# Windowed attention and two mixture layers on one core: gating products pinned in VectorE's queue, two a step, then four

## The chip, the core and the metric

The kernel runs on one core of a Trainium2 chip. The core has five engines with a queue of their own each: TensorE (PE in the rows; PEld is its weight load), VectorE (DVE), ScalarE (ACT), GpSimd (POOL) and SyncE (SP), which here issues nearly all DMA transfers. An engine takes its queue in order. The metric is device microseconds from start to end, the median of several runs.

## The reference

Three stages follow each other on 2304 tokens (4 sequences of 576) of 512 values:

```python
# 1. attention, 8 heads of 64: row i sees columns i-63 .. i
scores = where((rel >= 0) & (rel < 64), q @ k.T / 8, -1e9)
x = softmax(scores) @ v                      # tokens x 512
# 2. phase one: 512 -> 2048 -> 512
h = x @ w_in
g = where(h >= 1, h, where(h <= -1, 0, (h + 1)**2 / 4))
x = g @ w_out
# 3. phase two: 8 experts, each 512 -> 1024 -> 512, one for a token
logits = x @ w_gate                          # tokens x 8
e = argmax(logits); p = softmax(logits)[e]
out = p * (maximum(x @ w1[e], 0) @ w2[e])
```

## The kernel before

**Precision.** Matrices are split into a high and a low part, `hi` and `lo`; a product is three passes (hi hi, hi lo, lo hi), so that each operand needs a conversion on ScalarE and a subtraction on VectorE or GpSimd.

**Phase one.** Tokens lie in seven blocks of 256 or 384. A step is one of 16 slices of 128 hidden values for one block: `layer1` (L435), 12 products at L440 into the PSUM tile `h`, of which there are two; `act_g` (L447), a chain of six passes by turns on ScalarE and VectorE: L449 (ScalarE), L450 (VectorE), L451 (ScalarE), L452 (VectorE, the last that reads `h`), L455 (ScalarE, `ghi`), L456 (VectorE, `glo`); and, two steps later, `layer2` (L471), nine products at L475. The code walks over steps in the loop at L990. A step has two slots, `run_slot` at L1002 and L1021, into which other work is put: attention of later blocks, and what follows.

**Phase two.** All tokens are first sent through one expert, the one chosen most often among the first 128 tokens (`choose`, L607: its number `pi` goes to SyncE, which then loads that expert's weights as `er`; L642 converts them on ScalarE, L643 subtracts on GpSimd). Six blocks of 384 tokens take eight steps each: `layer1`, then `act_relu` (L461) with L464 on ScalarE and L465 on VectorE, then `layer2`, and `evac2` (L653), which scales with the gate's weight `GW` on ScalarE (L657) and writes to the output. `prep` (L901) fetches each block's input transposed (`tt`), joins its halves in `xj` and splits it (L910 on ScalarE, L911 on GpSimd). Tokens that belong to another expert are gathered after `route` and `pick` (L660, L724), put through their own expert (weights `wl`, again L642 and L643; first product L784), and scattered over the output.

**The gating products.** Logits are made on VectorE, one product of 128 tokens with one column of `w_gate` at a time: 18 tiles x 8 experts = 144 calls of `gate_logit` (L565), each a multiply with a running sum (`junk`) and a read of the accumulator (`Lg`); the trace has both under L569. The first call of a tile loads its rows, `xg`, of which two buffers exist. `gate_until(s, n)` (L928) puts the next n products into slot s; behind a tile group's last product follow `gate_finish` (L589), behind the first tile's also `choose`, and behind the last tile's `route` and `pick`. Slots from the start of phase one's last block get three products at first (RATE0), then two (RATE1, and RATE2 in phase two); a step has two slots, so four a step.

**What sets the order.** The code's order is not the queues' order. A scheduler reorders each engine's instructions when the program is built, by its own estimate of when inputs are there. A product needs only its rows and `w_gate`, so it can move up to where those are thought to have landed: in the queue before, products fill gaps between the passes of the activation chains of earlier steps as well.

Of the kernel before, what the change touches and what calls it, by code (L numbers as in the profile page):

```python
# [30 lines left out]
FAR = 32768.0  # L31
MAXT = NTILE + E - 1
RATE0 = 3
RATE1 = 2
RATE2 = 2
LA = 0
SPN = 8
# [73 lines left out]
def kernel(  # L111
# [14 lines left out]
    nc = tc.nc  # L126
# [423 lines left out]
    def load_rows(t, tag):  # L550
        r = Z["p2"].tile([P, DM], F32, tag=tag, name=tag, bufs=2)
        nc.sync.dma_start(r, x2s[t * P:t * P + P])
        return r
# [11 lines left out]
    def gate_logit(t, e):  # L565
        if e == 0:
            xg[t] = load_rows(t, "xg")
        junk = Z["p2"].tile([P, DM], BF16, tag="junk", name="junk")
        nc.vector.tensor_tensor_reduce(  # L569
            out=junk, in0=xg[t], in1=Z["wgb"][:, e], scale=1.0, scalar=0.0,  # L570
            op0=ALU.mult, op1=ALU.add, accum_out=Z["L"][:, t, e:e + 1],
        )

    def first_max(src, dst, n):

# [301 lines left out]
    def at(s, fn, *a):  # L877
        slots.setdefault(s, []).append((fn, a))
# [39 lines left out]
    sl = base + 2 * seg0[NB - 1]  # L918
# [9 lines left out]
    def gate_until(s, n):  # L928

        for t, e in gq[:n]:  # L930
            at(s, gate_logit, t, e)
            if e == E - 1:
                if t == 0:
                    at(s, gate_finish, 0, 1)
                    at(s, do_choose)
                elif t % TB == TB - 1:
                    a0 = max(1, t - TB + 1)
                    at(s, gate_finish, a0, t + 1 - a0)
                if t == NTILE - 1:
                    at(s, route)  # L940
                    at(s + 1, do_pick)
        del gq[:n]

    e0 = base + 2 * S2
    for s in range(sl + 1, e0):
        gate_until(s, RATE0 if s < sl + 5 else RATE1)
    for s in range(e0, e0 + 2 * KF2 * (NB2 - 1)):
        gate_until(s, RATE2)
    assert not gq
# [81 lines left out]
    with tc.For_i(1, n_left, 1):  # L1031
        nc.vector.tensor_scalar(out=Z["pos"], in0=Z["pos"], scalar1=-float(P), scalar2=None, op0=ALU.add)
        nc.vector.tensor_scalar(out=Z["j"], in0=Z["j"], scalar1=1.0, scalar2=None, op0=ALU.add)
        ev, idx, s, xl = pick()
# [65 lines left out]
```

## Time and profile before

| | us |
|---|---|
| median of three runs (772.76, 773.0, 776.55) | 773.0 |
| the profiled execution | 774.57 |
| its span, first to last instruction | 772.8 |
| TensorE busy | 727.8 (94%) |
| VectorE busy | 519.5 (67%) |
| ScalarE busy | 417.3 (54%) |
| GpSimd busy | 207.3 (27%) |
| gating products on VectorE, 144 | 113.9 |

TensorE is busy for most of the span, so time is lost or won where it stands still or runs at its lower clock. The shares are means over stages: the last block of phase one lies at about 465 to 541 us, phase two from there to about 760. "Idle before" in a row is the time that an engine stood before the instructions of a group, and behind the arrow stands what ended that wait.

### The profile page before, as it was taken

The page shows a single profiled execution, that of the slowest core. Times are in us where ns is not written, and L with a number is a line of the kernel's source. Part 1 is how long each engine was busy: PE and PEld are TensorE (multiplying, and loading weights), DVE is VectorE, ACT ScalarE, POOL GpSimd, SP SyncE. Part 2 cuts the span into 40 slices and gives each one's busy share as a digit, 9 for nine tenths or more (in the row PEclk, how much of TensorE's full clock was granted, in tenths as well). Part 3 has the DMA queues.
Part 4 walks back from the last instruction along what each step waited for, and adds up shares of the span by engine and source line. Part 5 has one row for each costly group of instructions (what it writes and reads, how often), then busy time and mean ns, then how long its engine had stood idle before and what let it go on. Part 6 is the DMA issues. An engine that isn't in the chain of part 4 may idle for free. (4 is left out here: it accounts for less than half of the span.)

```text
span 772.8 us, 12584 instructions
## 1 busy us (share of the span) xinstructions
PE 727.8 (94%) x4507; PEld 635.4 (82%) x4507; DVE 519.5 (67%) x1163; ACT 417.3 (54%) x1031; POOL 207.3 (27%) x164
## 2 busy tenths in 40 slices
PE   6698999999999999999999999979999999899996
PEld 3587878888888899888988898768988988799885
DVE  5887988548777668865797398999979854111110
ACT  4777766576656767575677444555533335441212
POOL 2466643204421024300320001561220116520000
PEclk7599999999999999999999999999999999999999
DMA  8446830143432324532343314432353134510101
GB/s 322 158 144 211 281 117 27 56 143 102 146 108 91 117 62 121 152 90 76 82 157 83 149 28 136 145 115 55 127 86 99 33 99 121 155 35 14 42 1 52
DMA packets 66691, 83.78 MB, mean 108 GB/s; under 512 B 35671, under 2 KB 41559, under 8 KB 66498
## 3 DMA queue, kind: packets, MB, share of 16 engines
q1 hardware_dynamic: 66466, 82.52, 34.6%
q8 instruction: 36, 0.59, 0.3%
q0 software_dynamic: 160, 0.43, 0.2%
q14 instruction: 29, 0.24, 0.1%
HBM read 60.74 MB, written 14.42 MB: 97 GB/s over the span
## 5 line engine op out<-in xcount | busy, mean ns | idle before, releaser
L440 PE MATMUL h<-xT,wi 128*128 128x384 f32 (+1 forms) x1344 | 233.5, 322 | 15.8 <-DVE a L452 12.8
L440 PEld LDWEIGHTS h<-xT,wi 128*128 128x128 f32 x1344 | 211.4, 193 | 30.3 <-DVE a L452 21.3
L475 PE MATMUL acc<-wo,ghi 128*128 128x512 f32 x576 | 155.7, 398 | 0.3 <-ACT ghi L455 0.2
L475 PEld LDWEIGHTS acc<-wo,ghi 128*128 128x128 f32 x576 | 104.3, 190 | 16.7 <-ACT ghi L455 1.0
L569 DVE CUSTOM_DVE_ANT_0 junk<-xg,wgb 128x512 bf16<-128x512 f32 x144 | 113.9, 791 | 2.4 <-DMA xg<-x2s 0.6
L440 PE MATMUL h<-xT,we 128*128 128x384 f32 x576 | 110.9, 337 | 3.2 <-DVE glo L465 3.2
L440 PEld LDWEIGHTS h<-xT,we 128*128 128x128 f32 x576 | 102.0, 188 | 9.0 <-DVE glo L465 4.7
L465 DVE SCALAR_TENSOR_TENSOR glo<-h,ghi 128x384 fp32r<-128x384 f32 x48 | 26.6, 554 | 93.2 <-ACT ghi L464 93.2
L475 PE MATMUL acc<-wo,glo 128*128 128x512 f32 x288 | 85.9, 395 | 0.6 <-DVE glo L456 0.5
L475 PE MATMUL acc<-we,ghi 128*128 128x512 f32 x288 | 79.3, 395 | 2.3 <-ACT ghi L464 2.2
L451 ACT ACTIVATE a<-a 128x384 f32<-128x384 f32 (+1 forms) x112 | 53.0, 474 | 50.6 <-DVE a L450 50.3
L456 DVE TENSOR_TENSOR glo<-a,ghi 128x384 fp32r<-128x384 f32 (+1 forms) x106 | 64.8, 612 | 21.4 <-ACT ghi L455 20.6
L455 ACT ACTIVATE ghi<-a 128x384 fp32r<-128x384 f32 (+1 forms) x112 | 53.0, 475 | 42.9 <-DVE a L452 42.0
L449 ACT ACTIVATE a<-h,half 128x384 f32<-128x384 f32 (+1 forms) x112 | 58.8, 525 | 30.5 <-PE h L440 29.1
L452 DVE TENSOR_TENSOR a<-h,a 128x384 f32<-128x384 f32 (+1 forms) x112 | 55.5, 497 | 26.1 <-ACT a L451 25.1
L450 DVE TENSOR_SCALAR a<-a 128x384 f32<-128x384 f32 (+1 forms) x112 | 48.9, 437 | 26.3 <-ACT a L449 26.1
L475 PEld LDWEIGHTS acc<-wo,glo 128*128 128x128 f32 x288 | 53.2, 188 | 13.5 <-DVE glo L456 1.9
L464 ACT ACTIVATE ghi<-h 128x384 fp32r<-128x384 f32 x48 | 23.1, 484 | 75.6 <-PE h L440 63.1
L475 PEld LDWEIGHTS acc<-we,ghi 128*128 128x128 f32 x288 | 52.8, 188 | 10.9 <-ACT ghi L464 2.4
L264 POOL TENSOR_TENSOR qs<-qk,qs 64x512 fp32r<-64x512 f32 x16 | 21.8, 1364 | 132.7 <-ACT qs L257 99.7
L911 POOL TENSOR_TENSOR xT<-xj,xT 128x256 fp32r<-128x256 f32 x36 | 30.5, 855 | 86.8 <-ACT xT L910 86.8
L643 POOL TENSOR_TENSOR we<-er,we 128x512 fp32r<-128x512 f32 x16 | 24.1, 1515 | 95.3 <-ACT we L642 95.3
(170 smaller groups left out, 979.8 us busy)
## 6 DMA issues: line engine op xcount, KB each, us to landing
qk<-in_qk_dram SPq DMA_DIRECT2D x21, 640.0 KB, 3.9
vt<-in_vv_dram SPq DMA_DIRECT2D x32, 256.0 KB, 2.8
er<-in_w_dram SPq DMA_DIRECT2D x32, 256.0 KB, 2.9
wraw<-in_wi_dram SPq DMA_DIRECT2D x14, 512.0 KB, 4.5
wraw<-in_wo_dram SPq DMA_DIRECT2D x14, 512.0 KB, 6.0
xg<-x2s SPq DMA_DIRECT2D x18, 256.0 KB, 2.7
out_dram<-y SPq DMA_DIRECT2D x18, 256.0 KB, 2.3
qk<-in_qq_dram SPq DMA_DIRECT2D x11, 320.0 KB, 3.2
```

The lines of the kernel that those rows point to most:

```text
L440: nc.tensor.matmul(h[:, :n], w[:, wa, k * P:k * P + P], x[:, xa, k, :n], start=(i == 0), stop=(i == 3 * KD - 1),)
L449: nc.scalar.activation(a[:, :n], h[:, :n], ACTF.Relu, scale=0.5, bias=half[:, 0:1])
L450: nc.vector.tensor_scalar(out=a[:, :n], in0=a[:, :n], scalar1=1.0, scalar2=None, op0=ALU.min)
L451: nc.scalar.activation(a[:, :n], a[:, :n], ACTF.Square)
L452: nc.vector.tensor_tensor(out=a[:, :n], in0=h[:, :n], in1=a[:, :n], op=ALU.max)
L455: nc.scalar.activation(hi[:, :n], a[:, :n], ACTF.Copy)
L456: (nc.gpsimd if pool else nc.vector).tensor_tensor(out=lo[:, :n], in0=a[:, :n], in1=hi[:, :n].bitcast(F32), op=ALU.subtract)
L465: nc.vector.scalar_tensor_tensor(out=lo[:, :n], in0=h[:, :n], scalar=0.0, in1=hi[:, :n].bitcast(F32), op0=ALU.max, op1=ALU.subtract,)
L475: nc.tensor.matmul(a, ga[:, t * P:t * P + P], w[:, wa], start=(first and j == 0), stop=(last and j == 2),)
L569: nc.vector.tensor_tensor_reduce(out=junk, in0=xg[t], in1=Z["wgb"][:, e], scale=1.0, scalar=0.0, op0=ALU.mult, op1=ALU.add, accum_out=Z["L ...
L643: nc.gpsimd.tensor_tensor(out=w[:, 1], in0=raw, in1=w[:, 0].bitcast(F32), op=ALU.subtract)
L911: (nc.vector if 2 * t + i in PL_V else nc.gpsimd).tensor_tensor(out=lo, in0=r, in1=hi.bitcast(F32), op=ALU.subtract)
```

## The change

Three edits. RATE1 falls from 2 to 1, so a step of phase one's last block gets two products instead of four; the slots that get three are one fewer (nine products instead of twelve). RATE2 stays at 2, four a step in phase two. And each product is pinned: `keep_in_program_order` gives it an edge of order, without a wait, to the instruction that the code issued last on VectorE. It can't move up past that one any more, but instructions that the code issues later may still move ahead of it.

```diff
-RATE1 = 2
+RATE1 = 1
 RATE2 = 2
@@ gate_logit
-        nc.vector.tensor_tensor_reduce(
+
+        tc.keep_in_program_order(nc.vector.tensor_tensor_reduce(
             out=junk, in0=xg[t], in1=Z["wgb"][:, e], scale=1.0, scalar=0.0,
             op0=ALU.mult, op1=ALU.add, accum_out=Z["L"][:, t, e:e + 1],
-        )
+        ))
...
     for s in range(sl + 1, e0):
-        gate_until(s, RATE0 if s < sl + 5 else RATE1)
+        gate_until(s, RATE0 if s < sl + 4 else RATE1)
     for s in range(e0, e0 + 2 * KF2 * (NB2 - 1)):
         gate_until(s, RATE2)
```

Behind the added empty line, line numbers of the kernel after are one higher from L569 on. No instruction of the five engines is added or removed by it but those that wait.

In VectorE's queue, before, one step in the middle of phase one's last block reads as follows. Each product is two rows, `junk,Lg` and `Lg`; L450, L452 and L456 are the step's activation chain.

```order
L450 TENSOR_SCALAR a<-a 128x384
L569 ISA junk,Lg<-xg,wgb 128x512
L569 ISA Lg 128x1
L452 TENSOR_TENSOR a<-h,a 128x384
L569 ISA junk,Lg<-xg,wgb 128x512
L569 ISA Lg 128x1
L569 ISA junk,Lg<-xg,wgb 128x512
L569 ISA Lg 128x1
L456 TENSOR_TENSOR glo<-a,ghi 128x384
L569 ISA junk,Lg<-xg,wgb 128x512
L569 ISA Lg 128x1
```

In the same queue after, at the next step of that block:

```order
L450 TENSOR_SCALAR a<-a 128x384
L570 ISA junk,Lg<-xg,wgb 128x512
L570 ISA Lg 128x1
L452 TENSOR_TENSOR a<-h,a 128x384
L456 TENSOR_TENSOR glo<-a,ghi 128x384
L570 ISA junk,Lg<-xg,wgb 128x512
L570 ISA Lg 128x1
L450 TENSOR_SCALAR a<-a 128x384
L570 ISA junk,Lg<-xg,wgb 128x512
L570 ISA Lg 128x1
L452 TENSOR_TENSOR a<-h,a 128x384
```

Four products a step have become two there. Over the whole queue, 77 products stand ahead of phase two's first L465 before, and 36 after; three of them stay at the early place, then four steps have none.

The second place is the choice of the common expert, in the same queue. Before, its last row, `pi`, stands inside the chain of the block's second step, next to the evacuation of the block ahead of it (L500, L162):

```order
L500 COPY xrow<-acc 128x512
L452 TENSOR_TENSOR a<-h,a 128x384
L569 ISA junk,Lg<-xg,wgb 128x512
L569 ISA Lg 128x1
L584 TENSOR_TENSOR poh<-ct,m_5354 128x8
L630 TENSOR_SCALAR pi<-m_5354 128x1
L162 COPY pl<-xrow 128x512 x2
L593 TENSOR_REDUCE gmx<-Lg 128x2
L569 ISA junk,Lg<-xg,wgb 128x512
L569 ISA Lg 128x1
L456 TENSOR_TENSOR glo<-a,ghi 128x384
```

After, it stands three chains further on, behind a whole chain that has no product in it:

```order
L450 TENSOR_SCALAR a<-a 128x384
L452 TENSOR_TENSOR a<-h,a 128x384
L456 TENSOR_TENSOR glo<-a,ghi 128x384
L620 TENSOR_REDUCE pcm<-cps 128x1
L621 TENSOR_SCALAR pcs<-cps,pcm 128x8
L580 SCALAR_TENSOR_TENSOR sc<-pcs,ct 128x8
L584 TENSOR_REDUCE m_5354<-sc 128x1
L585 TENSOR_TENSOR poh<-ct,m_5354 128x8
L631 TENSOR_SCALAR pi<-m_5354 128x1
L570 ISA junk,Lg<-xg,wgb 128x512
L570 ISA Lg 128x1
L450 TENSOR_SCALAR a<-a 128x384
```

So the weights of that expert are asked for about three steps later, and on ScalarE the 16 conversions at L642 (L643 after) move by as much; the order there has them between the passes of nine chains.

The third place is the middle of phase two in VectorE's queue, where the products end. Before, behind the 16th L465, only the end of the gate (L584, L603 and on) and the routing stand:

```order
L465 SCALAR_TENSOR_TENSOR glo<-h,ghi 128x384
L584 TENSOR_TENSOR OH<-ct,m_6982 128x24
L603 TENSOR_REDUCE gse<-gex 128x3
L663 TENSOR_TENSOR M<-OH,npoh 128x144
L604 TENSOR_SCALAR gse<-gse 128x3
L605 RECIPROCAL GW<-gse 128x3
```

After, behind the 17th L465 and ten more, four products stand as behind most others:

```order
L465 SCALAR_TENSOR_TENSOR glo<-h,ghi 128x384
L570 ISA junk,Lg<-xg,wgb 128x512
L570 ISA Lg 128x1
L570 ISA junk,Lg<-xg,wgb 128x512
L570 ISA Lg 128x1
L570 ISA junk,Lg<-xg,wgb 128x512
L570 ISA Lg 128x1
L570 ISA junk,Lg<-xg,wgb 128x512
L570 ISA Lg 128x1
L465 SCALAR_TENSOR_TENSOR glo<-h,ghi 128x384
```

The last product follows the 27th L465 instead of the 15th, and routing and the leftover expert's weights follow it. In SyncE's queue the loads of `xg` move with the products: at the ends of phase two's first two blocks, three of them stand in a row behind the block's third evacuation to the output (L658, L659 after), where before, at the end of the first block, one stood ahead of the third evacuation and one behind it.

## Rows read from the trace of the kernel before

**Rows 1.** busy us (instructions) of each engine by stretch, granted clock, DMA share, GB/s
```profile
478.00:530.00 52.00, 43.18 (x197) 37.71 (x196) 50.98 (x110) 28.92 (x56) 28.47 (x21) 0.93 0.40 118
541.00:611.00 70.00, 67.74 (x338) 60.51 (x337) 63.69 (x187) 27.00 (x56) 12.26 (x13) 1.00 0.36 89
633.00:676.00 43.00, 39.75 (x211) 34.18 (x210) 13.45 (x28) 20.93 (x40) 25.36 (x23) 1.00 0.46 133
```

**Rows 2.** first-layer products on TensorE, 400 to 478 us, then 478 to 530 us
```profile
L440 PE MATMUL h<-xT,wi 128*128 128x384 f32 x207 | 39.9, 339 | 0.6 <-DVE a L452 0.6
...
L440 PE MATMUL h<-xT,wi 128*128 128x384 f32 x116 | 25.5, 374 | 8.8 <-DVE a L452 8.8
```

**Rows 3.** TensorE in order of time: start, us, line, tiles, count, idle and releaser
```profile
508.41 3.89 PE L440 MATMUL h<-xT,wi 128*128 128x384 f32 x12 [2.05 <-DVE a L452]
...
522.77 3.76 PE L440 MATMUL h<-xT,wi 128*128 128x384 f32 x12 [4.06 <-DVE a L452]
...
528.43 2.27 PE L440 MATMUL h<-xT,wi 128*128 128x384 f32 x12
...
532.62 2.27 PE L440 MATMUL h<-xT,wi 128*128 128x384 f32 x12
```

**Rows 4.** VectorE's groups, 440 to 478 us (three rows), then 478 to 530 us
```profile
L569 DVE CUSTOM_DVE_ANT_0 junk<-xg,wgb 128x512 bf16<-128x512 f32 x28 | 19.2, 685 | 0.7 <-DMA xg<-x2s 0.6
L456 DVE TENSOR_TENSOR glo<-a,ghi 128x384 fp32r<-128x384 f32 x9 | 5.0, 556 | 0.6 <-ACT ghi L455 0.6
L452 DVE TENSOR_TENSOR a<-h,a 128x384 f32<-128x384 f32 x9 | 5.0, 554 | 1.2 <-ACT a L451 1.2
...
L569 DVE CUSTOM_DVE_ANT_0 junk<-xg,wgb 128x512 bf16<-128x512 f32 x37 | 36.6, 989 | 0.3
L456 DVE TENSOR_TENSOR glo<-a,ghi 128x384 fp32r<-128x384 f32 x9 | 7.6, 842 | 0.0
L452 DVE TENSOR_TENSOR a<-h,a 128x384 f32<-128x384 f32 x9 | 4.9, 549 | 0.0
```

**Rows 5.** VectorE busy in products and accumulator reads alone, three stretches
```profile
440.00:478.00 38.00, 18.86 (x55) 1.00 0.28 98
478.00:530.00 52.00, 35.97 (x73) 0.93 0.40 118
...
546.10:611.50 65.40, 50.14 (x136) 1.00 0.36 89
```

**Rows 6.** choice of the expert, conversions of its weights, ScalarE waiting for them
```profile
L630 DVE TENSOR_SCALAR pi<-m x1: 147/147/147, 470.9 to 470.9; 128x1 int32<-128x1 f32 x1
...
L642 ACT ACTIVATE we<-er x16: 613/630/635, 478.2 to 523.2; 128x512 fp32r<-128x512 f32 x16
...
ACT we L642 <- DMA er<-in_w_dram: 7.3, 9, 2.0
```

**Rows 7.** page, part 5: the first ScalarE pass of an activation chain
```profile
L449 ACT ACTIVATE a<-h,half 128x384 f32<-128x384 f32 (+1 forms) x112 | 58.8, 525 | 30.5 <-PE h L440 29.1
```

**Rows 8.** TensorE's two longest stops in phase two
```profile
587.88 1.83 PE L440 MATMUL h<-xT,we 128*128 128x384 f32 x9 [1.54 <-DVE glo L465]
...
671.04 1.66 PE L475 MATMUL acc<-we,ghi 128*128 128x512 f32 x6 [2.21 <-ACT ghi L464]
```

**Rows 9.** GpSimd splits for phase two; leftover expert: conversions and first product
```profile
L911 POOL TENSOR_TENSOR xT<-xj,xT 128x256 fp32r<-128x256 f32 x36 | 30.5, 855 | 86.8 <-ACT xT L910 86.8
...
L642 ACT ACTIVATE wl<-er x16: 615/632/634, 633.5 to 674.7; 128x512 fp32r<-128x512 f32 x16
L784 PE MATMUL hl<-wl,xTl x24: 389/389/389, 750.5 to 756.6; 128*128 128x512 f32 x24
```

**Rows 10.** row loads for products; ScalarE evacuating phase two, first block
```profile
DMA to landing us min/median/max: 2.5/2.7/8.7
...
585.93 1.27 ACT L657 ACTIVATE y<-acc,GW 128x512 f32<-128x512 f32 x2
...
592.31 0.69 ACT L657 ACTIVATE y<-acc,GW 128x512 f32<-128x512 f32 x1 [4.73 <-DMA out_dram<-y]
```

## The prediction

> **What bounds the kernel now.** The first view to read is busy time by stretch, since the page's shares mix a stage that runs TensorE without a break with one that does not. From 541 to 611 us TensorE is busy 67.74 of 70 us, but from 478 to 530 us only 43.18 of 52, at a granted clock of 0.93, while VectorE is busy 50.98 of those 52 [rows 1]. What TensorE waits for there is in its groups: 8.8 us of idle time stand before the first-layer products, all put down to L452, the VectorE step that last reads the product's PSUM tile; in the 78 us before 478 it is 0.6 us [rows 2]. In order of time the two longest stops are 2.05 and 4.06 us, and the twelve products behind them took 3.89 and 3.76 us against 2.27 [rows 3]: part of them ran at the lower of the two clock levels (1.2 GHz, not 2.4), which costs 1.62 + 1.49 = 3.1 us more. **The stretch loses 8.8 + 3.1 = 11.9 us**, the largest stop of the program's second half; the others are 2.3 us in 541 to 611 and 3.25 us in 633 to 676 [rows 1].
>
> Why VectorE is full there is in its groups. Before 478 a gating product takes 685 ns and L456 556; from 478 to 530, 989 and 842, while L452, which reads PSUM, stays at 554 and 549 [rows 4]. In that stretch GpSimd works 28.47 us (converted weights of the common expert, mostly) [rows 1]. So the two engines delay each other: 37 x 0.304 + 9 x 0.286 = 13.8 us of VectorE's time are that delay. And 37 products lie in 116/12 = 9.7 steps, 3.8 a step, where the code as written asks for four: they are not late, they are simply more than fits.
>
> [...]
>
> **The change, part by part.** No instruction is added or removed: 144 products stay, and each is free on VectorE only where something else holds the end. Three things move.
>
> (1) *Products leave the last block of phase one.* In VectorE's queue 77 stand ahead of the first L465 before, 36 now. With products and reads together, 35.97 us / 36.5 = 0.985 us each in the full stretch and 18.86 / 27.5 = 0.686 before it [rows 5]. The rest of VectorE's work in the full stretch is 50.98 - 35.97 = 15.0 us for 9.7 steps, 1.55 a step, delays included. A step that TensorE runs freely lasts 532.62 - 528.43 = 4.19 us [rows 3]. Before: 3.8 x 0.985 + 1.55 = 5.3 us a step, which is 1.1 over, as the rows show. Now the weight conversions lie beside nine steps whose queue holds 4, 4, 2, 2, 1, 3, 2, 2, 3 products, 23 in all: 23 x 0.985 + 9 x 1.55 = 36.6 us against 9 x 4.19 = 37.7. VectorE just fits. If instead GpSimd's whole 13.8 us of delay stays, whoever suffers it, it is 23 x 0.686 + 9 x (0.554 + 0.556 + some 0.25 for L450 where it overlaps) + 13.8 = 41.8, 4.1 over.
> Some of this is paid ahead of time by slack. After a first-layer product ends at about 530.7 its PSUM tile is wanted again one step and a second-layer product later, at about 536.8: 6.1 us. The chain to L452 takes two ScalarE passes of about 0.53 [rows 7], L450, L452 (0.55) and one product between, about 2.7 us. That leaves an estimated 3.4 us. The first two of the nine steps, with four products, overrun by 4 x 0.985 + 1.55 - 4.19 = 1.3 us each, which the slack holds if nothing else is late.
>
> Something is: the choice of the expert. The three products that start early stand where they stood, but the fourth is now behind L456 of the block's second step, so the eighth comes later and with it the choice (L631, `pi`), from ahead of that L456 to after the L456 three steps on: about three steps, 13 us. Before, it took 478.2 - 470.9 = 7.3 us from the choice to the first converted weight [rows 6]. ScalarE's order puts that conversion one activation chain after `pi` now, ahead of the next L449, so ScalarE stands some 2 us for the transfer, and L449 with all behind it. ScalarE waited 7.3 us for such weights in the stretch before too [rows 6], where VectorE hid it. I take **3 us as what is left** of the 11.9 (ends: 0, everything inside the slack; 9, three quarters of it). Gain 8.9. No gap of 2 us should be left, so the lower clock level goes as well. The weights themselves are not late: the last of the 16 lands some 13 us later than 523, when phase two's first block has barely begun, and its eighth second-layer weight is wanted some nine steps further on.
>
> (2) *Products enter phase two.* 108 remain after its first activation, four a step, and last to the 27th of 48 steps rather than the 15th: twelve steps longer, less the 9 us gained, so to about 652 us in place of 611. Free of GpSimd a step's VectorE work is 4 x 0.737 (50.14 / 68 [rows 5]) + 0.55 = 3.5 us of 4.19: it fits. It does not where GpSimd splits the next block's input, six instructions of 855 ns a block [rows 9]: the 2.3 us lost in 541 to 611 lie there, 1.54 of them at one stop that waits for L465 [rows 8]. That stretch held two such groups; the longer one holds four. At their mean of 1.1 us, two more cost **2 us** (ends: 0, as the group that cost almost nothing; 4.5, both at the dearer price).
>
> (3) *Routing and the leftover expert's weights come some 41 us later.* Before, these 16 conversions ran from 633.5 to 674.7 and their first reader at 750.5 [rows 9], 76 us of cover for the last. It shrinks to 76 - 41 = 35 us, less the gain, 26; nothing is paid. If the cover were gone, TensorE would stand at the end for what is missing. The stretch's own loss (3.25 us, of which 2.21 is ScalarE behind a weight transfer [rows 8]) moves with it: 16 conversions are now spread between about as many activations; I take it unchanged, 2 us either way.
>
> **Sum.** The profiled execution took 774.57 us: 774.57 - 8.9 + 2.0 = 767.7. It lies 1.6 above the median of the three runs (773.0), so a median run should lie between 766.1 and 767.7; I say **767.0 us**.
>
> **Rivals.** *VectorE stays full.* The 13.8 us of delay stay with GpSimd's work, the two four-product steps find no slack, and 9 of 11.9 remain: 774.57 - 2.9 + 2 = 773.7. For it: 41.8 against 37.7 above. Against: fewer products mean fewer collisions, and at 478 VectorE was still able to wait.
>
> *ScalarE takes VectorE's place.* Its order packs the 16 conversions into 8.4 steps, 35.2 us; before, they took 45.0 (478.2 to 523.2) [rows 6], 9.8 more, less 3.4 of slack, 6.4 lost. 774.57 - 11.9 + 6.4 + 2 = 771.1. For it: nine waits for the transfer already. Against: the leftover expert's 16 took 41.2 us [rows 9] with VectorE empty, so part of the 45 was not the transfer.
>
> *GpSimd holds VectorE for its full length.* The twelve splits beside added products would each hold VectorE 0.855 us, 10.3 us in all, against (4.19 - 3.5) x 8 = 5.5 us of room in the eight steps beside them: 4.8 lost where I took 2, which gives 770.5. For it: the products' mean of 0.989 us is made of some at 0.68 and some far above [rows 4]. Against: over the full stretch 13.8 of GpSimd's 28.47 us were lost, about half. The Trainium skill, page "SBUF — State Buffer", section "Who interferes with whom", has the full length as its rule: whoever comes second waits the other's whole instruction out. By that rule alone it would be this rival; the trace agrees for single instructions and not for the sum.
>
> *Slower: SyncE's queue makes the pinned products wait.* At the ends of phase two's first two blocks the queue now holds three row loads behind the third evacuation to the output; before, at the one such place, loads stood between. The third evacuation came 6.4 us after the first [rows 10], held by an output transfer. A row load behind it lands 2.7 us later, at most 8.7 [rows 10]; with two row buffers a tile's products last two steps, 8.4 us, so products stand still for what goes beyond that, L465 behind them, and TensorE once the 3.4 us of slack are gone. At 8.7 it is 6.4 + 8.7 - 8.4 - 3.4 = 3.3 us a place; where both buffers come late, twice that, 6.6, at two places 13.2: 774.57 - 6.9 + 13.2 = 780.9. It makes the kernel slower from (6.9 + 3.9) / 2 = 5.4 us a place on. Against: before, products waited 0.6 us for a load in all [rows 4].
>
> That the change does not do what it says is no rival: the built queues show it.
>
> **How the numbers follow.** Forecast 0.66, VectorE still full 0.10, ScalarE 0.08, full-length blocking 0.07, slower by SyncE 0.09. Range 761 to 775: the low end is nothing left and nothing paid in phase two, against a median run (774.57 - 1.6 - 11.9 = 761.1); the high end 9 left and 4.5 paid, likewise (774.57 - 1.6 - 2.9 + 4.5 = 774.6). Half a percent (about what a measurement of this kernel can tell from no change) is 3.9 us: faster means under 769.1, which is nine tenths of the forecast, 0.60; the rest of it and the three rivals in between, 0.31; slower 0.09.
>
> **What would show it.** Right: from the choice on to phase two, first-layer products wait for L452 under 4 us in all, the clock is 1.0, the mean product is nearer 0.8 us; products end near 650; the leftover expert's conversions end before 720. Wrong: VectorE over 97% busy in the steps with weight conversions (first rival); idle VectorE there with ScalarE waiting for `er` (second); products waiting for `xg` at the ends of phase two's first two blocks, near 577 and 610 (the slower one).

## The result and the profile after

The kernel after takes **767.11 us** (median, 766.86 to 767.65) beside 773.31 of the kernel before in the same comparison (772.76 to 776.55). The ratio is 0.9895, 95% interval 0.9871 to 0.9918: faster by about 1%. The profiled execution took 767.65 us (span 765.9) against 774.57 (span 772.8), 6.9 us less.

Its busy time by stretch follows, in the columns of [rows 1]. The choice of the expert (`pi`) is made at 485.8 now, so the stretch with the weight conversions is 488 to 540.

```profile
440.00:478.00 38.00, 38.00 (x192) 34.38 (x191) 18.55 (x45) 16.71 (x31) 0.00 (x0) 1.00 0.21 81
478.00:488.00 10.00, 10.00 (x52) 8.93 (x51) 8.03 (x33) 3.91 (x9) 0.00 (x0) 1.00 0.37 106
488.00:526.00 38.00, 33.04 (x162) 28.33 (x161) 32.11 (x65) 21.92 (x43) 20.62 (x16) 1.00 0.38 118
526.00:540.00 14.00, 12.81 (x63) 10.82 (x62) 10.42 (x24) 8.07 (x18) 6.88 (x7) 1.00 0.34 95
540.00:600.00 60.00, 57.38 (x284) 50.44 (x283) 51.31 (x142) 25.12 (x50) 10.88 (x12) 1.00 0.37 97
600.00:655.00 55.00, 55.00 (x280) 50.08 (x279) 51.17 (x141) 22.80 (x45) 10.16 (x12) 1.00 0.33 87
655.00:680.00 25.00, 25.00 (x131) 21.89 (x130) 14.98 (x63) 7.04 (x16) 5.82 (x6) 1.00 0.17 49
680.00:720.00 40.00, 40.00 (x210) 35.38 (x209) 13.43 (x25) 16.48 (x31) 20.31 (x18) 1.00 0.35 112
```

The granted clock is 1.00 in each, where it was 0.93. VectorE is busy 32.11 of 38 us beside the conversions (85%), where it was 50.98 of 52 (98%). From 655 to 720, with the leftover expert's conversions, TensorE stands nowhere.

All that the view of waits lists for TensorE from 440 us to the end, by engine and line (us in total, times, longest), stands in two rows:

```profile
PE h L440 <- DVE a L452: 5.9, 4, 2.5
PE h L440 <- DVE glo L465: 2.6, 3, 1.5
```

In order of time (columns of [rows 3]), the four stops that make the 5.9 us are these:

```profile
500.50 2.37 PE L440 MATMUL h<-xT,wi 128*128 128x384 f32 x12 [0.63 <-DVE a L452]
...
506.54 2.36 PE L440 MATMUL h<-xT,wi 128*128 128x384 f32 x12 [1.58 <-DVE a L452]
...
522.62 2.35 PE L440 MATMUL h<-xT,wi 128*128 128x384 f32 x12 [2.54 <-DVE a L452]
...
537.01 2.36 PE L440 MATMUL h<-xT,we 128*128 128x384 f32 x12 [1.14 <-DVE a L452]
```

The products behind them take 2.35 to 2.37 us, and the granted clock is 1.00 throughout. Before, the stretch lost 8.8 us of waiting and 3.1 us of clock [rows 2, 3]; now it loses 5.9 and none.

VectorE's groups from 488 to 526 us (columns of [rows 4]) show what became of the delay by GpSimd:

```profile
L570 DVE CUSTOM_DVE_ANT_0 junk<-xg,wgb 128x512 bf16<-128x512 f32 x19 | 18.3, 961 | 0.1
L450 DVE TENSOR_SCALAR a<-a 128x384 f32<-128x384 f32 x7 | 6.9, 992 | 1.5 <-ACT a L449 1.5
L456 DVE TENSOR_TENSOR glo<-a,ghi 128x384 fp32r<-128x384 f32 x7 | 4.3, 618 | 1.8 <-ACT ghi L455 1.8
L452 DVE TENSOR_TENSOR a<-h,a 128x384 f32<-128x384 f32 x6 | 3.3, 553 | 2.0 <-ACT a L451 2.0
```

The products are nearly as slow as before (961 ns, 989 before), L456 is almost free of delay (618 against 842), and **L450 takes 992 ns**, where the kernel after needs a median of 361 for it from 440 to 478 us. Before, from 478 to 530 us, it was delayed far less:

```profile
L450 DVE TENSOR_SCALAR a<-a 128x384 f32<-128x384 f32 x10 | 4.8, 477 | 0.7 <-ACT a L449 0.7
```

So more of the delay now falls on a link of the activation chain itself.

The choice and the conversions, for [rows 6] and [rows 9]:

```profile
L631 DVE TENSOR_SCALAR pi<-m x1: 147/147/147, 485.8 to 485.8; 128x1 int32<-128x1 f32 x1
...
L643 ACT ACTIVATE we<-er x16: 602/626/633, 490.1 to 535.3; 128x512 fp32r<-128x512 f32 x16
...
L785 PE MATMUL hl<-wl,xTl x24: 389/389/389, 743.6 to 749.8; 128*128 128x512 f32 x24
L643 ACT ACTIVATE wl<-er x16: 622/632/633, 672.5 to 710.1; 128x512 fp32r<-128x512 f32 x16
```

### The profile page after: what moved, and what is told of

The parts are those of the page before. It is cut to its first block, busy times and chain, and to the rows that moved or that the text cites. A ratio compares the mean times of both kernels' runs of the same rounds, so it can differ in the third digit from the quotient of the medians.

```text
span 765.9 us, 12576 instructions
## 1 busy us (share of the span) xinstructions
PE 725.1 (95%) x4507; PEld 631.0 (82%) x4507; DVE 526.6 (69%) x1163; ACT 417.2 (54%) x1031; POOL 205.7 (27%) x164
## 5 line engine op out<-in xcount | busy, mean ns | idle before, releaser
L440 PE MATMUL h<-xT,wi 128*128 128x384 f32 (+1 forms) x1344 | 230.0, 318 | 12.3 <-DVE a L452 8.8
L440 PEld LDWEIGHTS h<-xT,wi 128*128 128x128 f32 x1344 | 207.9, 190 | 27.7 <-DVE a L452 17.7
L475 PE MATMUL acc<-wo,ghi 128*128 128x512 f32 x576 | 155.5, 398 | 0.5 <-ACT ghi L455 0.4
L475 PEld LDWEIGHTS acc<-wo,ghi 128*128 128x128 f32 x576 | 103.7, 189 | 16.7 <-ACT ghi L455 1.2
L440 PE MATMUL h<-xT,we 128*128 128x384 f32 x576 | 110.7, 338 | 3.8 <-DVE glo L465 2.6
L570 DVE CUSTOM_DVE_ANT_0 junk<-xg,wgb 128x512 bf16<-128x512 f32 x144 | 111.6, 775 | 3.2 <-DMA xg<-x2s 0.4
L440 PEld LDWEIGHTS h<-xT,we 128*128 128x128 f32 x576 | 101.7, 188 | 10.1 <-DVE glo L465 4.7
L475 PE MATMUL acc<-wo,glo 128*128 128x512 f32 x288 | 85.8, 396 | 0.5 <-DVE glo L456 0.3
L456 DVE TENSOR_TENSOR glo<-a,ghi 128x384 fp32r<-128x384 f32 (+1 forms) x106 | 64.9, 613 | 30.5 <-ACT ghi L455 29.7
L451 ACT ACTIVATE a<-a 128x384 f32<-128x384 f32 (+1 forms) x112 | 53.1, 475 | 54.3 <-DVE a L450 54.0
L452 DVE TENSOR_TENSOR a<-h,a 128x384 f32<-128x384 f32 (+1 forms) x112 | 55.5, 497 | 33.6 <-ACT a L451 32.7
L475 PE MATMUL acc<-we,ghi 128*128 128x512 f32 x288 | 78.4, 395 | 0.0
L450 DVE TENSOR_SCALAR a<-a 128x384 f32<-128x384 f32 (+1 forms) x112 | 52.1, 465 | 32.8 <-ACT a L449 32.6
L475 PEld LDWEIGHTS acc<-wo,glo 128*128 128x128 f32 x288 | 53.1, 188 | 13.7 <-DVE glo L456 2.2
L465 DVE SCALAR_TENSOR_TENSOR glo<-h,ghi 128x384 fp32r<-128x384 f32 x48 | 26.6, 555 | 51.2 <-ACT ghi L464 51.2
L475 PEld LDWEIGHTS acc<-we,ghi 128*128 128x128 f32 x288 | 53.0, 188 | 8.2 <-ACT y L658 0.2
L912 POOL TENSOR_TENSOR xT<-xj,xT 128x256 fp32r<-128x256 f32 x36 | 30.9, 868 | 89.4 <-ACT xT L911 89.4
L644 POOL TENSOR_TENSOR we<-er,we 128x512 fp32r<-128x512 f32 x16 | 22.4, 1406 | 108.1 <-ACT we L643 108.0
```

Of the source, the lines that this page charges most:

```text
L440: nc.tensor.matmul(h[:, :n], w[:, wa, k * P:k * P + P], x[:, xa, k, :n], start=(i == 0), stop=(i == 3 * KD - 1),)
L450: nc.vector.tensor_scalar(out=a[:, :n], in0=a[:, :n], scalar1=1.0, scalar2=None, op0=ALU.min)
L451: nc.scalar.activation(a[:, :n], a[:, :n], ACTF.Square)
L452: nc.vector.tensor_tensor(out=a[:, :n], in0=h[:, :n], in1=a[:, :n], op=ALU.max)
L456: (nc.gpsimd if pool else nc.vector).tensor_tensor(out=lo[:, :n], in0=a[:, :n], in1=hi[:, :n].bitcast(F32), op=ALU.subtract)
L465: nc.vector.scalar_tensor_tensor(out=lo[:, :n], in0=h[:, :n], scalar=0.0, in1=hi[:, :n].bitcast(F32), op0=ALU.max, op1=ALU.subtract,)
```

## The experiments

**How a run's time is read.** In every run, what TensorE loses from 440 us on was added up in the profiled execution and taken from that execution's time. It is its waits, and, where the granted clock falls to 0.5, what groups of products take over the time of the same groups at 1.00 (the twelve at L440 over 2.27 us, the six at L475 over 1.55):

| kernel | profiled, us | waits, us | clock, us | time less losses |
|---|---|---|---|---|
| before | 774.57 | 14.2 | 3.2 | 757.2 |
| after | 767.65 | 8.5 | 0 | 759.2 |
| rates alone | 769.44 | 10.9 | 2.8 | 755.7 |
| pin alone | 770.51 | 11.3 | 3.3 | 755.9 |
| after, GpSimd without reads | 759.15 | 3.5 | 0 | 755.7 |
| before, GpSimd without reads | 766.8 | 7.4 | 0 | 759.4 |
| before, routing later | 773.76 | 13.1 | 3.3 | 757.4 |
| after, one product a step | 769.38 | 6.8 | 2.7 | 759.9 |
| after, choice early | 761.7 | 3.9 | 0 | 757.8 |
| after, subtraction on VectorE | 763.25 | 4.2 | 1.6 | 757.5 |
| both of these | 757.4 | 1.3 | 0 | 756.1 |

The last column stays within 4.2 us while the time moves by 17. So these two numbers are the account of a run, to about 2 us either way, and an edit has to be argued by them.

**1. The rates alone**, on the kernel before, without the pin:

```diff
-RATE1 = 2
+RATE1 = 1
-        gate_until(s, RATE0 if s < sl + 5 else RATE1)
+        gate_until(s, RATE0 if s < sl + 4 else RATE1)
```

> The kernel before with the two rates of the change (two products a step in phase one's last block, nine in the first slots), without the pin. In VectorE's queue 77 products still stand ahead of phase two's first L465, as before, since the scheduler moves them up. Theory (what counts is how many products stand beside the conversions of the common expert's weights): as before, 772 to 775 us. Rival (the lower rate itself spreads them): as the change, 767.

Measured: 771.27 us, ratio 0.9969 (0.9948 to 0.9991), just under the range expected. The scheduler moved the products up again: 77 stand ahead of phase two's first L465, as many as before. What TensorE waited for from 440 us on:

```profile
PE h L440 <- DVE a L452: 10.2, 6, 4.0
PE h L440 <- DVE glo L465: 0.7, 2, 0.3
```

One group of products again took 4.21 us behind a stop of 4.04, and the six at L475 behind it 2.37 where 1.55 is usual. So the stretch loses 10.2 + 2.8 = 13.0 us, no less than before (8.8 + 3.2 = 12.0). The number in the code alone does nothing for it. What the run gained lies in phase two: TensorE waits 0.7 us for L465 in place of 3.2. Both of these stops lie beside the leftover expert's weights, at 631 to 671 us, where before has them too and loses 3.25.

**2. The pin alone**, on the kernel after, with the old rates:

```diff
-RATE1 = 1
+RATE1 = 2
-        gate_until(s, RATE0 if s < sl + 4 else RATE1)
+        gate_until(s, RATE0 if s < sl + 5 else RATE1)
```

> The changed kernel with the rates of before (four a step in phase one's last block, twelve products in the first slots), pinned. In VectorE's queue 48 products stand ahead of phase two's first L465 (77 before, 36 with the change), but behind the choice of the expert they stand 3 to 5 a step, as before. Theory (number of products beside the conversions): the stretch loses 8 to 12 us of TensorE's time as before; routing comes some 13 steps' products later, so the loss at the leftover expert's weights may go as with the change (3 us): 769 to 773. Rival (the pin itself, that products stand behind their own step's chain): 767.

Measured: 771.35 us, ratio 0.9979 (0.9955 to 1.0002), no difference that can be told. Here 48 products stand ahead of the first L465, but three to five a step behind the choice, just where the conversions lie. VectorE is busy 51.48 of 53 us there (488 to 541), TensorE waited 9.9 us for L452, and the lower clock is back:

```profile
505.47 3.48 PE L440 MATMUL h<-xT,wi 128*128 128x384 f32 x12 [2.74 <-DVE a L452]
...
540.01 3.81 PE L440 MATMUL h<-xT,we 128*128 128x384 f32 x12 [2.96 <-DVE a L452]
```

The two edits are worth 0.2 to 0.3% each and 1.05% together. The rate says how many products a step should have, the pin makes it so.

**3 and 4. The kernels after and before without GpSimd's reads** for the common expert. GpSimd fills the low part of those weights with zeros, so that part of phase two's weights is left out; the 16 fills write only:

```diff
-        nc.gpsimd.tensor_tensor(out=w[:, 1], in0=raw, in1=w[:, 0].bitcast(F32), op=ALU.subtract)
+        if name == "we":
+            nc.gpsimd.memset(w[:, 1].bitcast(F32), 0.0)
+        else:
+            nc.gpsimd.tensor_tensor(out=w[:, 1], in0=raw, in1=w[:, 0].bitcast(F32), op=ALU.subtract)
```

> The changed kernel with GpSimd's 16 subtractions for the common expert's weights replaced by fills with zeros, which read nothing: the low part of those weights is left out. It takes GpSimd's delay off VectorE in that stretch and also frees the two raw weight buffers sooner. Theory (what is left, 5.9 us of waits for L452, is VectorE's products delayed by GpSimd): products there take 0.69 us, waits fall under 2 us, 762 to 764. Rival (ScalarE standing for the weights' transfers): products at 0.69 us, but waits of 4 us and more stay, 765 to 767.

> The kernel before with the same replacement (the low part of the common expert's weights is left out). Theory (3.8 products a step are too many only because GpSimd delays them: 3.8 x 0.69 + some 1.3 is 3.9 of 4.19 us): most of the 11.9 us goes, 763 to 766. Rival (ScalarE standing for transfers, or simply the number of products): 770 to 773.

Measured: after 760.14 us, ratio 0.9827 (0.9779 to 0.9874), against 0.9895 with the reads, a greater gain than the 762 to 764 us expected; before 765.35, ratio 0.9889 (0.9844 to 0.9934), within the range. In the kernel before so changed, VectorE's groups from 478 to 507 us, the time of its weight conversions, are these:

```profile
L569 DVE CUSTOM_DVE_ANT_0 junk<-xg,wgb 128x512 bf16<-128x512 f32 x22 | 15.5, 703 | 0.1
L456 DVE TENSOR_TENSOR glo<-a,ghi 128x384 fp32r<-128x384 f32 x6 | 3.3, 557 | 4.2 <-ACT ghi L455 4.2
...
L450 DVE TENSOR_SCALAR a<-a 128x384 f32<-128x384 f32 x6 | 2.2, 367 | 0.7 <-ACT a L449 0.7
```

With 76 products ahead of phase two (77 with the reads), every instruction has its own length again (703, 557, 367 ns), and TensorE waits 2.4 us for L452 in place of 8.8 plus 3.1 of clock. So that many products were too much beside GpSimd's subtractions and are not beside its fills, as the prediction had it. In the kernel after, the wait for L452 falls from 5.9 to 2.8 us, not under 2 as expected. More than the reads changes, though. A fill takes 0.53 us where a subtraction takes 1.3 to 1.5, and it does not wait for the raw weights, so their buffers come free sooner: the conversions take 28.2 us from first to last where after has 45.2, and 27.8 where before has 45.0. How much of the gain each of these is was not taken apart.

**5. The kernel before with routing and the leftover expert 24 slots later**, the first instruction of routing pinned:

```diff
-        nc.vector.tensor_tensor(
+        tc.keep_in_program_order(nc.vector.tensor_tensor(
             out=M, in0=Z["OH"], in1=Z["npoh"].to_broadcast([P, NTILE, E]), op=ALU.mult
-        )
+        ))
...
-                    at(s, route)
-                    at(s + 1, do_pick)
+                    at(s + 24, route)
+                    at(s + 25, do_pick)
```

> The kernel before, with routing and the leftover expert's weights asked for 24 slots later (and the first routing instruction pinned); the products stand as before. It does alone what the change does to the leftover expert. Theory (the 3 us that the profile of before loses beside the leftover expert's conversions go because they move away from the split of the block ahead): 769 to 771 us, no stop of TensorE beside these conversions, the 11 to 12 us at phase one's last block unchanged. Rival (that loss comes and goes by itself): no change, 772 to 774.

Measured: 774.87 us, ratio 1.0005 (0.999 to 1.002), where 769 to 771 was expected. The loss moved with the weights. They were converted at 693 to 730 us, and beside them TensorE waited 2.8 us for L465 in two stops, where before loses 3.25 beside them. ScalarE and TensorE around the longer one:

```profile
723.98 0.63 ACT L642 ACTIVATE wl<-er 128x512 fp32r<-128x512 f32 x1 [1.59 <-DMA er<-in_w_dram]
724.51 0.47 ACT L464 ACTIVATE ghi<-h 128x384 fp32r<-128x384 f32 x1
...
725.63 1.83 PE L440 MATMUL h<-xT,we 128*128 128x384 f32 x9 [2.40 <-DVE glo L465]
```

The conversion waits for its transfer, and the activation that TensorE needs stands behind it. The kernel before shows the same, around its stop at 671.04 [rows 8]:

```profile
665.63 0.63 ACT L642 ACTIVATE wl<-er 128x512 fp32r<-128x512 f32 x1 [1.05 <-DMA er<-in_w_dram]
...
669.98 0.63 ACT L642 ACTIVATE wl<-er 128x512 fp32r<-128x512 f32 x1 [3.71 <-DMA er<-in_w_dram]
670.52 0.47 ACT L464 ACTIVATE ghi<-h 128x384 fp32r<-128x384 f32 x1
```

But the loss need not come. With the rates alone, at the same place in the program, the conversion at 661.47 waits 2.58 us and the four behind it 1.18 to 1.92, and TensorE loses 0.7 us beside all sixteen; in the kernel after, the longest wait is 3.25, ahead of the first conversion, and TensorE loses nothing. A single late transfer falls on a wanted activation or it doesn't.

**6. The kernel after with one product a step** in the last block:

```diff
-        gate_until(s, RATE0 if s < sl + 4 else RATE1)
+        gate_until(s, RATE0 if s < sl + 4 else RATE1 * (s % 2))
```

> The changed kernel with one product a step, not two, in phase one's last block: 23 stand ahead of phase two's first L465 (36 with the change), some 10 beside the conversions of the common expert's weights. Theory (the number of products there is what costs): waits for L452 fall from 5.9 to 2 to 3 us, 763 to 765. Against it: products end six or seven steps later, near 680 us, so the leftover expert's conversions end near 735 with its first product near 740; where that cover is gone TensorE stands at the end, 767 or more. Rival (ScalarE standing for transfers is what is left): waits of 5 us and more stay, 766 to 768.

Measured: 768.44 us (765.47 to 769.38), ratio 0.9921 (0.9896 to 0.9945), no better than after; the expectation missed. The stretch did what was expected, 3.0 us for L452 in place of 5.9. Phase two then had stops of its own:

```profile
PE h L440 <- DVE a L452: 3.0, 4, 1.2
PE acc L475 <- ACT y L658: 1.7, 1, 1.7
PE h L440 <- DVE glo L465: 1.1, 2, 0.9
PE tp L558 <- DMA xl<-x2s,idx: 1.0, 1, 1.0
```

Products now end at 665 us, and the leftover expert's weights are converted at 684 to 721, into the evacuation of phase two's fifth block (L658). There TensorE stands three times from 715.7 to 720.5 us, 3.0 us in all, and from 719.5 to 726.3 the granted clock is 0.5, the lower level:

```profile
720.51 1.22 PE L475 MATMUL acc<-we,ghi 128*128 128x512 f32 x2 [1.73 <-ACT y L658]
...
723.56 2.12 PE L440 MATMUL h<-xT,we 128*128 128x384 f32 x6
```

In the kernel after the same six products take 1.23 us, and the groups that take 8.10 us here, from 720.51 on, take 5.39. So this kernel loses 2.9 us less than after in the stretch, 1.7 less at L465 early in phase two, and 5.7 more beside the leftover expert's weights. The late end of its products undoes the gain, though not by the way that was expected: the first product of the leftover expert (L785, at 745.4) still has 24 us of cover.

**7. The kernel after with the choice at its early place:** the first tile's eight products go into one slot, and one into every slot behind it, 37 ahead of phase two (36 in after):

```diff
-        gate_until(s, RATE0 if s < sl + 4 else RATE1)
+        gate_until(s, E if s == sl + 1 else RATE1)
```

> The changed kernel with all eight products of the first tile at the early place where three stood, so that the expert is chosen about five steps sooner; two a step from then on. The same number of products (37) lies ahead of phase two's first L465, but some 30 of them beside or after conversions that start sooner. Theory (products beside conversions are what costs, two a step just do not fit): 4 to 7 us of waits stay, 766 to 768. Rival (the late choice, which makes ScalarE stand ahead of L449, is what is left): waits fall under 3 us, 763 to 765.

Measured: 761.73 us, ratio 0.9849 (0.9832 to 0.9866), where 766 to 768 was expected: 5.4 us under after by the medians, 3.6 by the ratios to before. `pi` is at 464.9 and the conversions at 469.3 to 511.0, all of them inside phase one. TensorE waits for one thing from 440 us on:

```profile
PE h L440 <- DVE a L452: 3.9, 4, 1.7
```

The wait lies between the two that were expected (4 to 7, under 3), and the time below both. ScalarE stood for the weights longer than in after (10.3 us against 6.8 from 440 to 560 us), so the sum of that standing does not explain the 2.0 us in the stretch. VectorE has fewer products beside the conversions, 16 from 470 to 515 us, 1.5 a step of 4.19 us, where after has 19 from 488 to 526, 2.1 a step; and they take 752 ns, where after has 961. L450 is still delayed:

```profile
L450 DVE TENSOR_SCALAR a<-a 128x384 f32<-128x384 f32 x9 | 8.1, 901 | 0.5 <-ACT a L449 0.5
```

Why the 2.6 us of phase two went as well was not tested.

**8. The kernel after with the common expert's subtraction on VectorE:**

```diff
-        nc.gpsimd.tensor_tensor(out=w[:, 1], in0=raw, in1=w[:, 0].bitcast(F32), op=ALU.subtract)
+        (nc.vector if name == "we" else nc.gpsimd).tensor_tensor(
+            out=w[:, 1], in0=raw, in1=w[:, 0].bitcast(F32), op=ALU.subtract)
```

> The changed kernel with the 16 subtractions for the common expert's weights on VectorE instead of GpSimd. It adds 16 x 0.55 = 9 us to VectorE and takes away GpSimd's delay there; products are issued behind these subtractions in the code, so that 21, not 36, stand ahead of phase two's first L465. Theory (GpSimd's delay of VectorE costs more than its work would): waits for L452 under 3 us, 760 to 764. Rival (VectorE is full by its own work): waits of 5 us and more, 767 to 770.

Measured: 762.59 us, ratio 0.9862 (0.9838 to 0.9887), as the theory said. One subtraction takes a median of 692 ns there, where GpSimd in the kernel after takes 1304. VectorE gets 11 us more to do and TensorE waits 1.8 us for L452. Work added to the engine that had been full made the kernel faster than after, by 4.5 us (medians) or 2.6 (ratios): from 485 to 526 us L450 is back at 354 ns and L456 at 554, and VectorE is busy 25.66 of 41 us with the subtractions among it. But the edit moved the products as well: 21 stand ahead of phase two and none starts beside the conversions (490.9 to 521.9). So this run alone does not tell the two apart; the next one does. Its waits for L465 (2.4 us) and 1.6 us of lower clock lie beside the leftover expert's weights or right behind them.

**9. Both, 7 and 8:**

> Kernel after with both edits at once: the eight products of the first tile in one early slot (761.7 us alone, TensorE waits for L452 3.9 us) and the 16 subtractions of the common expert's weights on VectorE (762.6 us alone, waits for L452 1.8 us and for L465 2.4). Theory (what is left in the stretch after the choice has two sources, the late choice and the two-input reads of GpSimd beside VectorE's): the edits add, waits for L452 fall to 0 to 2, no wait for L465, 757 to 760 us. Rival (both edits free VectorE of the same few collisions, and 16 x 0.69 = 11 us of subtractions then lie beside the one product a slot): the edits do not add, waits for L452 stay at 2 to 5, 761 to 764 us.

Measured: **758.11 us** (756.61 to 758.98), ratio 0.9788 (0.9765 to 0.9811), the fastest of all. The gains add as far as these runs can tell: 5.4 and 4.5 us alone and 9.0 together by the medians, 3.6, 2.6 and 8.3 by the ratios. As in the run with the early choice alone, 37 products stand ahead of phase two, and there are 20 from 470 to 515 us where that run has 16 (beside the conversions themselves 13 in 37 us, where that run has 16 in 42). So the wait for L452, 1.3 us in place of 3.9, hardly fell for want of products beside the conversions: the subtractions cost less on VectorE than their delay from GpSimd did. VectorE's groups from 470 to 515 us, and all that TensorE waited for from 440 us on:

```profile
L570 DVE CUSTOM_DVE_ANT_0 junk<-xg,wgb 128x512 bf16<-128x512 f32 x20 | 13.7, 683 | 0.0
L644 DVE TENSOR_TENSOR we<-er,we 128x512 fp32r<-128x512 f32 x14 | 9.7, 691 | 4.4 <-ACT we L643 4.2
...
L450 DVE TENSOR_SCALAR a<-a 128x384 f32<-128x384 f32 x11 | 3.9, 353 | 0.0
```

```profile
PE h L440 <- DVE a L452: 1.3, 2, 1.0
```

## Why the prediction came out

The time was forecast at 767.0 us and came out at 767.1, and the mechanism for the last block, products leaving a stretch in which GpSimd's subtractions delay VectorE, is what the runs show. But three terms of the sum were off, one to one side and two to the other, and 3.25 us of the gain lie where none was forecast.

**(1) The last block, forecast a gain of 8.9, measured 6.0.** The clock part came out, 3.1 us gone, but not for its reason: no gap of 2 us was to be left, and one of 2.54 was, without the lower level behind it. The waits were to be 3 us, "under 4" in the list of what would show it, and are 5.9. The step that failed is the one from fewer products to fewer collisions. Products were to come nearer 0.8 us; from the choice on to phase two they take 878 ns (486 to 541 us; 923 before, from 471 on), and beside the conversions 961. Against the lengths ahead of the stretch (685, 556, and 361 ns for L450), VectorE's delay from 488 to 526 us is 19 x 0.276 + 7 x 0.631 + 7 x 0.062 = 10.1 us, beside 20.62 us of GpSimd's work. Before, it was the 13.8 us of the prediction and 1.2 on L450, 15.0 beside 28.47. That is about half of GpSimd's time in both (0.49 and 0.53). So the premise of the first rival (the delay stays) was the better one. Its conclusion (VectorE stays full) was not: with 19 products in 38 us, where before had 37 in 52, VectorE is busy 85% and not 98%, and the delay no longer adds up from step to step.

What is left falls on single steps. The working gave L450 some 0.25 us a step and saw the delay on products and L456; L450 takes 0.99 us, 0.63 of them delay. Ahead of the stop of 0.63 us stands an L450 of 1.44 us, ahead of that of 1.58 an L450 of 1.36 and a product of 1.77, and ahead of that of 2.54 an L450 of 0.89 and products of 1.72 and 1.76. The stop of 1.14 us, at 537.01, is of the kind that the prediction named: ScalarE stood for a weight transfer with the chain, here its L451, behind it.

```profile
535.32 0.63 ACT L643 ACTIVATE we<-er 128x512 fp32r<-128x512 f32 x1 [2.29 <-DMA er<-in_w_dram]
535.86 0.51 ACT L451 ACTIVATE a<-a 128x384 f32<-128x384 f32 x1
```

So ScalarE's standing accounts for 1.14 of the 5.9 us in these rows, where the prediction made it the cause of all 3. That GpSimd's subtractions delay L450 too is shown by the two kernels without them: it takes 357 ns with fills (six from 488 to 517 us) and 354 with the subtractions on VectorE. In the first of them no L450 met a fill, so it does not show whether a fill would delay it; in the kernel before with fills one L450, at 498.76, met one and took 442 ns. What the early choice gains in the stretch is not taken apart: its products are fewer and faster, its L450 is as slow.

**(2) Phase two, forecast a loss of 2.0, measured about none.** L465 cost 2.6 us from 540 to 600 in after, against 2.3 from 541 to 611 before, and nothing from 600 to 655, where the other two groups of GpSimd's splits lie and VectorE is busy 51.17 of 55 us. The step that failed was to price a group of splits at the mean of two. The third rival, GpSimd at its full length, is out by the same rows (its 4.8 us of loss did not come; the single products that it argues from, 0.68 us and far above, are in the trace, up to 1.79 us, but not in rows 4, which give their mean). So is the slower one: all products together waited 0.4 us for their rows.

**(3) The leftover expert, forecast unchanged, measured a gain of 3.25.** The cover was read rightly (conversions end at 710.1, 33 us ahead of the first reader, 26 to 35 forecast). The step that failed is to carry the loss of 3.25 us along with the weights as a fixed term. It can move with them (2.8 us in experiment 5), but it need not come at all (0.7 us at the old place in experiment 1, none in the kernel after). All that TensorE loses from 541 us on, waits and clock, spreads as widely: 5.5 us before, 5.0 without GpSimd's reads and 4.7 with routing later, the three kernels with the old gating code; with other gating code 0 (choice early), 0.7 (rates alone), 1.4 (pin alone), 2.6 (after), 4.0 (subtraction on VectorE) and 6.5 (one product a step). What in the schedule brings it is not settled. In three kernels (routing later, one product a step, subtraction on VectorE) the conversions last into the evacuation of phase two's fifth block, and TensorE stands there; in the kernel after, with the choice early and with both edits they end 7 to 9 us ahead of it, and it does not. No run tests that, and the stop of 2.21 us before lies elsewhere. So a forecast can only give this loss a spread.

**The sum.** The gains are 6.0 + 3.25 less 0.3, 8.9 us, and the profiled executions differ by 6.9. Of the 2 us between, 1.1 lie ahead of the stretch (the first product, at its old place in the queue, starts at 445.9 us and not 444.8); 0.9 were not found. The forecast of 6.9 net was met by luck: 2.9 too much in (1) stood against 1.7 and 3.25 too little in (2) and (3), and those 2 us. The range of 761 to 775 was made mostly by the right unknown, what is left in the last block.

## What to carry to other kernels

Where two engines delay each other, count the delay per instruction of the slower engine and ask which instruction of the other it will meet: here, with fewer products a step, about the same share of GpSimd's time was lost on VectorE, and more of it on the critical chain. Giving the whole piece of work to one engine can be cheaper although that engine is the fuller one. A rate written in the code is only a wish while the scheduler may move instructions up; look at the built queue before pricing it. Losses at a single stop that waits for one transfer belong into the range of a forecast, not into its sum.

## What the runs showed of the hardware

**L450 has one input and is delayed all the same.** The prediction's sum counted GpSimd's delay on products and on L456, which have two inputs in SBUF each. GpSimd from 516.6 us on, and VectorE in the same time, both of the kernel after:

```profile
516.60 1.70 POOL L644 TENSOR_TENSOR we<-er,we 128x512 fp32r<-128x512 f32 x1
518.49 0.96 POOL L912 TENSOR_TENSOR xT<-xj,xT 128x256 fp32r<-128x256 f32 x1 [0.19 <-ACT xT L911]
519.43 1.37 POOL L644 TENSOR_TENSOR we<-er,we 128x512 fp32r<-128x512 f32 x1
```

```profile
517.13 1.72 DVE L570 CUSTOM_DVE_ANT_0 junk<-xg,wgb 128x512 bf16<-128x512 f32 x1
...
518.78 0.89 DVE L450 TENSOR_SCALAR a<-a 128x384 f32<-128x384 f32 x1
519.59 1.76 DVE L570 CUSTOM_DVE_ANT_0 junk<-xg,wgb 128x512 bf16<-128x512 f32 x1
```

Each of the three on VectorE starts while GpSimd is at work, and each ends 0.2 to 0.6 us after it (518.85, 519.67 and 521.35 against 518.30, 519.45 and 520.80). L450 takes 0.89 us, 0.53 over its length, for a split of 0.96 at L912. This is the stop of 2.54 us at 522.62: L452 starts at 522.01, behind the two delayed products, the delayed L450 and one more product of 0.69 us.

The Trainium skill, page "SBUF — State Buffer", section "Who interferes with whom", has a rule that the sum leaves out: `tensor_scalar` can enter a mode that takes the port pair shared with GpSimd, and then it contends as well. These rows agree. It also says that a VectorE instruction with two SBUF inputs does not contend with a GpSimd instruction that only writes; the zero fills agree (in the kernel before with fills, products take 703 ns and L456 557).

**A longer stop is not always followed by the lower clock.** In the kernel after the products behind 2.54 us took 2.35 us, and with the pin alone those behind 2.39 took 2.38. Before, those behind 2.05 us took 3.89 [rows 3], and with routing later those behind 2.33 took 3.65. With one product a step the granted clock fell to 0.5 behind three shorter stops, of 1.03, 0.23 and 1.73 us. So the length of the one stop does not decide it.
